# Transposing the first keys as fp32 on TensorE, a contiguous token-mixing weight in batch 0, and an uneven split of the last output piece

## The chip, the cores and the metric

The kernel runs on one core of a Trainium2 chip. A core has TensorE (PE, the matmul array), VectorE (DVE), ScalarE (ACT), GpSimd (POOL) and SyncE (SP, which here only issues transfers), each with its own instruction stream, run in order. SP, ACT and POOL start DMA transfers. Matmuls write PSUM, eight banks of 128 partitions by 2 KB; [...]everything else lives in SBUF. The metric is the device time of one execution in microseconds (us): 292.88 for the kernel before, the median of three runs from 292.81 to 293.12.

## What is computed

Performer attention with positive random features, and on its output one token- and channel-mixing MLP block. With 8 batches, 8 heads, 576 tokens, head size 64 and 128 features:

```python
def phi(x):                                  # x scaled by D ** -0.25
    proj = np.einsum('bhsd,md->bhsm', x, omega)
    sq = np.sum(x * x, axis=-1, keepdims=True) / 2.0
    h = proj - sq
    h = h - np.max(h, axis=-1, keepdims=True)
    return np.exp(h) / np.sqrt(m)
kv = np.einsum('bhsm,bhsd->bhmd', k_p, v)
z = np.sum(k_p, axis=2)
x = num / den                                # num = q_p kv, den = q_p z + 1e-6; heads side by side: 576 x 512
h = np.maximum(xt @ w_tok1, 0.0) @ w_tok2    # xt = x transposed, w_tok 576 x 256 and 256 x 576
u = x + h.transpose(0, 2, 1)
h2 = np.maximum(u @ w_ch1, 0.0) @ w_ch2      # 512 x 1536 and 1536 x 512
out = u + h2
```

Inputs and output are fp32; the kernel computes in fp16 with fp32 sums in PSUM.

## The kernel before

**Tiling.** Of each batch's 576 tokens, 512 are the main part, four blocks j of 128, and 64 are the tail; the tails of two batches share one set of 128 partitions. In SBUF, partition p of block j holds token 4p + j, since loads put four neighbouring tokens on one partition. Heads go in four pairs, hp = 0 to 3; the output of a pair fills 128 of the 512 columns, called db.

**The order.** A planner in the kernel (class `Planner`) takes jobs with an engine, an assumed cost, a due key, the jobs they depend on and the buffers that they take and give (six PSUM banks, one PSUM pair, rings of SBUF tiles). It writes out each engine's instructions once, in an order that follows from costs and keys; on the chip that order is fixed. The tables `KEYS`, `NEAR`, `HEAD` and `BY` hold the keys, and for batch 0 which engine (A for ScalarE, D for VectorE) takes which copy out of PSUM. Where PE would have nothing to do before the first channel mix, the planner inserts matmuls of zeros (L908).

**The opening, batch 0.** All that the change touches but the last piece lies here.
- `load_first` (L375) brings the fp32 keys in four transfers of two heads each, two issued by ACT and two by SP, into `first_k`, a view of the space that the weights `wc2` take later. A ScalarE copy (L381) casts each to fp16 in `nat`.
- `transposes` (L459) turns two heads with four TensorE transposes (L465): the data are the loaded weights and an identity is the moving operand. L470 (ACT) or L472 (DVE) copies the result from PSUM to `kT`. `tail_transposes` (L485, L489) does this for the tail tokens. POOL makes the fp16 identity at L387.
- For each pair: `kp` (L611) multiplies keys by the features, L494 on ACT takes the exponential, L637 and L639 on DVE the maximum per token and its reciprocal, L644 on POOL scales v, `kv` (L657, L664) sums over tokens, and L672 copies the sums out. `qp` (L625) and its exponentials (L494) do the same for the queries, `num` (L691, L693) forms numerator and denominator, and L700 and L701 on DVE divide them into x. Where `BY["no"]` has an A, L710 takes the reciprocal on DVE and ACT does the division in five pieces (L713).
- `token_mix_first` (L760) then takes each db: the first token matmul t1 (L771, L772), a relu (L778 on ACT or L780 on DVE), and a group of PE work that forms u transposed in one bank: four identity matmuls (L787) put x in, transposed, and two matmuls with w_tok2 as the moving operand (L789) add the second token product. L793 copies the bank to `uT`. L789 reads w_tok2 through a view that reorders its columns,

```python
    def w2_of(tb, j=None):
        rows = w2[:, tb, 0:SM].rearrange("p (c j) -> p j c", j=NJ)
        return rows if j is None else rows[:, j, :]
```

so that bank column 128j + c is token 4c + j.
- The first `channel_mix` matmuls (L828, L830) start when `uT` is there; from then on PE has dense work. L822 is the first channel product, L839 its relu on ACT, L855 the second, L864 on DVE adds u (L861 copies for batch 0, whose u is added by L853 on PE), and L869 stores the block.

**The body.** Batches 1 to 7 run the same steps interleaved with the channel mix of the batch before. From batch 2 on, q and k are cast by a POOL transfer to DRAM (L354) and transposed by a DMA on SP's queue (L362).

**The end.** A ninth channel mix takes the tails. Its last block j = 3 is done in two column halves of 256, each with 12 matmuls L855, one add L864 and two stores L872 of 64 partitions, one issued by SP and one by ACT.

Of the kernel before, what the change touches and what calls it, by code (L numbers as in the profile page):

```python
# [9 lines left out]
FP32 = mybir.dt.float32  # L10
# [6 lines left out]
KEYS = {"a": -1.383, "as": 0.1, "t": -0.936, "ts": 0.381, "gv": 2.163, "lt": -2.027, "lv": -2.126, "to": -1.882, "tt": 0.315, "ks": 0.333, "km": 0.498, "vs": -0.625, "l1": -2.543, "kt": -0.025}  # L17
NEAR = {"1": {"a": -1.493, "as": 0.086, "t": -1.525, "ts": 0.0, "gv": -0.107, "km": -1.714, "vs": -0.23, "kt": -0.097}, "2": {"a": -1.272, "as": 0.154, "t": -0.7, "ts": 0.142, "gv": 1.686, "km": 3.516, "vs": 1.881, "lv": -1.598, "lt": -2.533, "kt": 0.06}}
HEAD = {"kp": [-3.838, -3.822, -3.798, -3.404], "ke": [-2.728, -2.927, -2.827, -2.727], "km": [-4.011, -3.564, -4.193, -4.006], "vs": [-3.332, -3.487, -3.03, -3.14], "qp": [-3.503, -3.403, -3.303, -3.203], "qe": [-3.328, -3.374, -3.028, -3.128], "kv": [-3.45, -3.145, -2.92, -3.05], "ko": [-3.015, -2.969, -3.397, -2.755], "n": [-3.199, -3.199, -3.182, -3.099, -2.999, -2.999, -2.899, -2.899], "no": [-3.34, -3.34, -3.24, -3.058, -3.14, -4.038, -3.04, -2.3], "ktm": -3.64, "kt": -5.015, "kte": -3.991, "qt": -3.751, "qte": -4.062, "kx": [-6.595, -5.9, -5.8, -5.7], "kxo": [-6.013, -7.195, -5.8, -5.71], "ktx": -6.15, "ktxo": -5.5, "qx": [-5.449, -2.792], "qxo": [-4.557, -3.081], "qtx": -5.58, "qtxo": -3.371, "t1": [-0.475, -0.755, -0.539, -0.445], "re": [-0.554, -0.394, -0.244, -0.084], "ut": [-0.17, -0.48, -0.32, -0.64], "uo": [-0.453, -0.293, -0.302, 0.017], "vbd": -8.94, "w1": -9.59, "w1t": -9.68, "w2t": -8.94, "wa": -8.32, "wb": -8.79, "w2": -8.13}
BY = {"kx": "DDDD", "ktx": "A", "qx": "AD", "qtx": "D", "ko": "ADDA", "re": "AADA", "uo": "DAAA", "no": "DDDDDDDD"}  # L20
# [157 lines left out]
def kernel(  # L178
# [12 lines left out]
    nc = tc.nc  # L191
# [3 lines left out]
    DM = H * D  # L195
# [20 lines left out]
    def sb(shape, dt, name):  # L216
        return pool.tile(shape, dt, name=name)
# [13 lines left out]
    omT = sb([P, M], FP16, "omT")  # L231
    ident16 = sb([P, P], FP16, "ident16")
# [71 lines left out]
    def dma(eng, key, wire, fn, deps=(), take=(), give=(), cost=None):  # L304
        cost = (0.75 if eng == "POOL" else 0.45) if cost is None else cost
        job = add(eng, cost, key, fn, deps, take, give, wire=wire)
        if eng == "POOL":
            job.after = issued[-1] if issued else None
            issued.append(job)
        return job  # L310
# [64 lines left out]
    def load_first(h0, h1, eng, key, to):  # L375
        def go():
            (nc.sync if eng == "SP" else nc.scalar).dma_start(
                out=first_k[:, h0:h1, :], in_=k[0, h0:h1, 0:SM, :].rearrange("h (p j) d -> p h (j d)", j=NJ))
        got = dma(eng, key, 0.37 * (h1 - h0), go, cost=0.47)
        def cast():  # L380
            (nc.vector.tensor_copy if to == "DVE" else nc.scalar.copy)(out=nat["k", 0][:, h0:h1, :], in_=first_k[:, h0:h1, :])  # L381
        job = add(to, 0.6 if to == "DVE" else 0.5, key + 0.1, cast, deps=[got])
        for h in range(h0, h1):
            ld["k", 0, h] = job

    def identities():
        make_identity(nc, ident16)  # L387
    j_ident = add("POOL", 0.45, -9.9, identities)
    j_om = [dma("SP", -9.95, 0.1, lambda: nc.sync.dma_start(out=omega_nat, in_=omega))]
    load_first(0, 2, "ACT", -9.9, "ACT")  # L390
    load_first(2, 4, "SP", -9.9, "ACT")
    load_first(4, 6, "ACT", -9.7, "ACT")
    load_first(6, 8, "SP", -9.7, "ACT")
# [27 lines left out]
    def w2_of(tb, j=None):  # L421
        rows = w2[:, tb, 0:SM].rearrange("p (c j) -> p j c", j=NJ)
        return rows if j is None else rows[:, j, :]
# [35 lines left out]
    def transposes(b, w, h0, h1, key, on_act=False, key_out=None):  # L459
        name = ("t", w, b, h0)  # L460
        def go():
            ps, ident = bank16(name), ident16
            for i in range(2 * (h1 - h0)):
                h, pr = h0 + i // 2, i % 2
                nc.tensor.transpose(ps[:, i * P : (i + 1) * P], nat[w, b][:, h, pr * P : (pr + 1) * P], ident)  # L465
        def out_():
            n = h1 - h0
            ps = bank16(name)[:, 0 : n * R].rearrange("p (h r) -> p h r", h=n)
            if on_act:
                nc.scalar.copy(out=rows_of(b, w)[:, h0:h1, 0:R], in_=ps)  # L470
            else:
                nc.vector.tensor_copy(out=rows_of(b, w)[:, h0:h1, 0:R], in_=ps)  # L472
        take = [("bank", name)]
        take.append((w + "T", b))
        t = add("PE", mm(2 * (h1 - h0), P) * 1, key, go, deps=[ld[w, b, h0], j_ident], take=take)
        e = add("ACT" if on_act else "DVE", 0.1 + 0.21 * (h1 - h0) if on_act else 0.16 + 0.13 * (h1 - h0), key if key_out is None else key_out, out_, deps=[t], give=[("bank", name)])
        for h in range(h0, h1):
            tr[w, b, h] = e
# [281 lines left out]
    def token_mix_first(b, key, step, jx):  # L760

        jrs, uT = [], []
        for db in range(ND):
# [20 lines left out]
            def ut_(n2=n2, cols=cols):  # L784
                ps, x, r1 = bank(n2), t_x[place("x", b)], t_r1[place("r1", b)]
                for j in range(NJ):
                    nc.tensor.matmul(ps[:, j * P : (j + 1) * P], x[:, j, cols], ident16, start=(j == 0), stop=False, skip_group_check=True)  # L787
                for tb in range(NT):
                    nc.tensor.matmul(ps, r1[:, tb, cols], w2_of(tb), start=False, stop=(tb == NT - 1), skip_group_check=True)  # L789
# [23 lines left out]
    def channel_mix(c, key, jt):  # L813
# [27 lines left out]
        for j in range(NJ):  # L841
            last = c == B and j == NJ - 1
            for hf in range(2 if last else 1):
                n = ("h4", c, j, hf)
                cols = slice(hf * (DM // 2), (hf + 1) * (DM // 2)) if last else slice(0, DM)
                prev = None
                for part in range(3):
# [8 lines left out]
                    prev = add("PE", mm(4, 256 if last else 512) + (mm(4, P) if c == 0 and part == 2 else 0.0), key + 0.5 + 0.5 * (3 * j + part) / 12 + 0.2 * hf, c2,  # L856
# [8 lines left out]
                jo = add("DVE", 0.4 if last else 0.69, k2, oadd, deps=[prev], take=[("o", (c, j))], give=[("bank", n)] + ([("u", c)] if 0 < c < B else []))  # L865
                def store(j=j, cols=cols, last=last):
                    o = t_o[place("o", (c, j))]
                    if c < B:
                        nc.sync.dma_start(out=out[c, 0:SM, :].rearrange("(p j) d -> p j d", j=NJ)[:, j, :], in_=o)  # L869
                    else:  # L870
                        for i in range(2):
                            (nc.scalar if j >= 2 and i else nc.sync).dma_start(out=out[2 * j + i, SM:S, cols], in_=o[i * ST : (i + 1) * ST, cols])  # L872
# [68 lines left out]
```

## Time and profile before

| | us |
|---|---|
| median of three runs | 292.88 |
| the profiled execution | 292.57 |
| its span, first to last instruction | 290.8 |
| PE busy | 283.9 |
| ACT, DVE, POOL busy | 155.9, 145.3, 90.6 |
| first L828 | 28.07 |
| end of the last add (L864) | 287.43 |

The span is shorter than the time of its execution by what lies before the first and after the last instruction that the profile counts. A busy time of PE overlaps neighbouring matmuls, since the ends of matmuls are modelled; the chain of work that ended last steps from start to start and shows what a matmul really adds. In a line of a group, "out<-in" names tiles, then come shapes, types and count, busy time in us and mean in ns, and the idle time before it with what ended it. In a line of the chain the columns are start, length in us and the work.

### The profile page before, as it was taken

How to read it: one execution, taken by the hardware profiler on the slowest of the kernel's cores; microseconds unless marked ns; L12 is line 12 of the kernel's file. 1: busy time of each engine (PE TensorE's matmuls, PEld its weight loads, DVE VectorE, ACT ScalarE, POOL GpSimd, SP SyncE). 2: the span in 40 equal slices, each digit the busy share in tenths (PEclk: the TensorE clock that was granted, in tenths of full speed). 3: DMA queues.
4: the chain of work that ended last, by engine and by line, in shares of the span. 5: the costliest groups of instructions: out<-in, count | busy, mean ns of one | idle time of the engine just before them, and what ended most of it. 6: DMA issues, size and time to landing. Idle time of an engine off the chain costs nothing.

```text
span 290.8 us, 5502 instructions
## 1 busy us (share of the span) xinstructions
PE 283.9 (98%) x2210; PEld 141.7 (49%) x2210; DVE 145.3 (50%) x269; ACT 155.9 (54%) x305; POOL 90.6 (31%) x115
## 2 busy tenths in 40 slices
PE   7899999999999999999999999999999999999994
PEld 3465454445544544465445544554455444444443
DVE  4885843558449533756567446646465242111011
ACT  5963992098457553865466636753765501621700
POOL 8995740128006501550165014601421000000000
PEclk9999999999999999999999999999999999999998
DMA  8999999699964996999769976897711033003004
GB/s 192 193 197 195 202 228 172 98 246 175 177 108 108 186 152 125 180 171 202 113 129 182 197 114 113 159 221 115 152 72 39 0 72 147 0 18 144 2 20 124
DMA packets 75737, 39.57 MB, mean 136 GB/s; under 512 B 54976, under 2 KB 70720, under 8 KB 75328
## 3 DMA queue, kind: packets, MB, share of 16 engines
q0 software_dynamic: 24304, 17.43, 41.2%
q1 hardware_dynamic: 50624, 21.01, 32.3%
q10 hardware_dynamic: 784, 0.79, 0.9%
q8 instruction: 17, 0.28, 0.4%
q14 instruction: 8, 0.07, 0.1%
HBM read 35.88 MB, written 16.52 MB: 180 GB/s over the span
## 4 chain that ended last, share of the span: by engine, by line
PE 95%; ACT 3%; DVE 0%; issue 0%; DVEq 0%; ACTq 0%
PE bank L855 33%; PE bank L822 32%; PE bank L745 4%; PE bank L728 4%; PE bank L611 3%; PE bank L657 3%; PE bank L625 2%; PE pair L691 2%; PE bank L908 2%; ACT kp L494 1%; PE bank L789 1%; PE bank L803 1%; PE bank L664 1%; PE bank L465 1%; PE bank L729 1%; ACT qp L494 1%
## 5 line engine op out<-in xcount | busy, mean ns | idle before, releaser
L839 ACT ACTIVATE r<-bank 128x512 f16<-128x512 f32 x108 | 64.5, 602 | 69.8 <-PE bank L822 69.8
L855 PE MATMUL bank<-wc,r 128*128 128x512 f16 (+1 forms) x444 | 101.5, 374 | 0.0
L822 PE MATMUL bank<-uT,wc 128*128 128x512 f16 x376 | 89.5, 379 | 0.0
L855 PEld LDWEIGHTS <-r 128*128 128x128 f16 x444 | 40.8, 98 | 46.9 <-issue 5.1
L822 PEld LDWEIGHTS <-wc 128*128 128x128 f16 x424 | 39.5, 98 | 42.6 <-issue 0.5
L637 DVE TENSOR_REDUCE km<-kp 128x8 f16<-128x1024 f16 x32 | 38.7, 1209 | 9.4 <-ACT kp L494 9.2
L494 ACT ACTIVATE qp<-bank 128x512 f16<-128x512 f32 x64 | 35.2, 620 | 13.4 <-PE bank L625 13.4
L494 ACT ACTIVATE kp<-bank 128x512 f16<-128x512 f32 x64 | 34.4, 610 | 8.9 <-PE bank L611 8.9
L644 POOL TENSOR_TENSOR vs<-v,vs 128x512 f16<-128x512 f16 x32 | 33.4, 1055 | 16.1 <-DVE vs L639 12.1
L864 DVE TENSOR_TENSOR o<-u,bank 128x512 f32<-128x512 f16 x28 | 19.1, 681 | 28.1 <-PE bank L855 28.1
L571 POOL TENSOR_TENSOR vbd<-vt,vbd 128x1024 f16<-128x1024 f16 x7 | 13.4, 1919 | 33.2 <-DVE vbd L562 21.7
L365 POOL COPY ktt<-kT 128x256 f16<-128x256 f16 x6 | 2.4, 396 | 68.4 <-DMA kT<-k 68.4
L701 DVE TENSOR_TENSOR x<-pair,rc 128x640 f16<-128x640 f32 x28 | 23.1, 824 | 1.0
L748 DVE TENSOR_TENSOR u<-x,bank 128x512 f16<-128x512 f16 x28 | 17.4, 682 | 9.1 <-PE bank L745 9.1
L700 DVE RECIPROCAL rc<-pair 128x10 f32<-128x10 f32 x28 | 6.0, 216 | 26.9 <-PE pair L693 26.9
L691 PEld LDWEIGHTS <-qp 128*128 128x128 f16 x256 | 12.8, 98 | 6.1 <-issue 0.7
L736 DVE TENSOR_SCALAR r<-bank 128x512 f16<-128x512 f32 x7 | 4.8, 692 | 19.5 <-PE bank L729 19.5
L728 PE MATMUL bank<-x,w1m 128*128 128x512 f16 x56 | 14.4, 379 | 0.0
L657 PEld LDWEIGHTS <-kp 128*128 128x128 f16 x256 | 10.9, 98 | 5.3 <-ACT qp L494 0.9
L657 PE MATMUL bank<-vs,kp 128*128 128x65 f16 x256 | 13.0, 193 | 0.4 <-ACT qp L494 0.4
L745 PE MATMUL bank<-r,w 128*128 128x512 f16 x56 | 13.2, 379 | 0.0
L611 PE MATMUL bank<-omT,kT 64*128 64x128 f16 x256 | 12.5, 218 | 0.1
(102 smaller groups left out, 267.8 us busy)
## 6 DMA issues: line engine op xcount, KB each, us to landing
out_dram<-o SPq DMA_DIRECT2D x32, 256.0 KB, 2.5
q<-in_q_dram POOLq DMA_DIRECT2D x6, 576.0 KB, 6.5
k<-in_k_dram POOLq DMA_DIRECT2D x6, 576.0 KB, 10.2
wc<-in_moe_w_ch_dram POOLq DMA_DIRECT2D x4, 768.0 KB, 10.3
v<-in_v_dram POOLq DMA_DIRECT2D x6, 512.0 KB, 6.3
r<-in_q_dram POOLq DMA_DIRECT2D x4, 256.0 KB, 7.2
v<-in_v_dram POOLq DMA_DIRECT2D x4, 256.0 KB, 7.2
out_dram<-o SPq DMA_DIRECT2D x5, 128.0 KB, 2.3
```

What stands on the lines that cost most here:

```text
L494: nc.scalar.activation(out=out, in_=in_, func=AF.Exp, bias=0.0, scale=1.0)
L611: nc.tensor.matmul(ps[e][:, c : c + M], m[half[e], r, :], omT[half[e]], start=True, stop=True)
L637: nc.vector.reduce_max(out=mx, in_=kpv, axis=AX.X)
L644: nc.gpsimd.tensor_tensor(out=vs[:, :, 0:D], in0=t_v[place("v", b)][:, hh[0] : hh[0] + 2, :].rearrange("p h (j d) -> p (h j) d", d=D), in1 ...
L657: nc.tensor.matmul(ps[:, i, :], kpv[:, 2 * i + j // 2, j % 2, :], vs[:, i * NJ + j, 0 : D + 1], start=(i == 0 and j == 0), stop=False, ski ...
L701: nc.vector.tensor_tensor(out=t_x[place("x", b)][:, :, (2 * hp + hs[0]) * D : (2 * hp + hs[0] + n) * D].rearrange("p j (i d) -> p i j d", ...
L728: nc.tensor.matmul(ps, w1m[:, j, tb * P : (tb + 1) * P], x[:, j, :], start=(j == 0), stop=False)
L745: nc.tensor.matmul(ps, w2_of(tb, j), r1[:, tb, :], start=(tb == 0), stop=(tb == NT - 1))
L822: nc.tensor.matmul(ps, wc1[:, db, cb * P : (cb + 1) * P], moving(db), start=(db == 0), stop=(db == ND - 1))
L839: nc.scalar.activation(out=t_r3[place("r3", c)][:, cb, :], in_=bank(n), func=AF.Relu)
L855: nc.tensor.matmul(ps[:, cols], r3[:, cb, j * P : (j + 1) * P], wc2[:, cb, cols], start=(cb == 0), stop=(cb == NCB - 1))
L864: nc.vector.tensor_tensor(out=t_o[place("o", (c, j))][:, cols], in0=uu[:, cols], in1=bank(n)[:, cols], op=ALU.add)
```

## The change

It has three parts, and the planner's tables come with them.

1. Batch 0's w_tok2 is read as it lies. The identity matmuls L787 write the bank in steps of four columns instead, so that bank column t is token t; blocks j of `uT` are then 128 neighbouring tokens, and batch 0's output rows are stored in that order.
2. The ScalarE casts of batch 0's keys are gone. TensorE transposes the fp32 keys with an fp32 identity into an fp32 bank, and the DVE copy out of it casts to fp16. POOL makes the fp32 identity, and DVE copies it to fp16 for the other uses.
3. The last block's columns are split 384 and 128 instead of 256 and 256.

The tables change keys in `KEYS`, `NEAR` and `HEAD` (for batch 0 of `kp`, `qp`, `kxo`, `qxo` and `wb`), and in `BY` the tail keys' copy moves to DVE, the last pair's kv copy to DVE, the relus all to ACT, and the first head's division to ACT.

```diff
-BY = {"kx": "DDDD", "ktx": "A", "qx": "AD", "qtx": "D", "ko": "ADDA", "re": "AADA", "uo": "DAAA", "no": "DDDDDDDD"}
+BY = {"kx": "DDDD", "ktx": "D", "qx": "AD", "qtx": "D", "ko": "ADDD", "re": "AAAA", "uo": "DAAA", "no": "ADDDDDDD"}
...
-    def load_first(h0, h1, eng, key, to):
+    def load_first(h0, h1, eng, key):
...
-        got = dma(eng, key, 0.37 * (h1 - h0), go, cost=0.47)
-        def cast():
-            (nc.vector.tensor_copy if to == "DVE" else nc.scalar.copy)(out=nat["k", 0][:, h0:h1, :], in_=first_k[:, h0:h1, :])
-        job = add(to, 0.6 if to == "DVE" else 0.5, key + 0.1, cast, deps=[got])
+        job = dma(eng, key, 0.37 * (h1 - h0), go, cost=0.47)
...
-        make_identity(nc, ident16)
-    j_ident = add("POOL", 0.45, -9.9, identities)
+        make_identity(nc, ident32)
+    j_ident32 = add("POOL", 0.45, -9.9, identities)
+    j_ident = add("DVE", 0.2, -9.9, lambda: nc.vector.tensor_copy(out=ident16, in_=ident32), deps=[j_ident32])
...
-    def w2_of(tb, j=None):
-        rows = w2[:, tb, 0:SM].rearrange("p (c j) -> p j c", j=NJ)
-        return rows if j is None else rows[:, j, :]
+    def w2_of(tb, j):
+        return w2[:, tb, 0:SM].rearrange("p (c j) -> p j c", j=NJ)[:, j, :]
...
+        first = b == 0 and w == "k"
         def go():
-            ps, ident = bank16(name), ident16
+            ps = bank(name) if first else bank16(name)
+            what, ident = (first_k, ident32) if first else (nat[w, b], ident16)
             for i in range(2 * (h1 - h0)):
                 h, pr = h0 + i // 2, i % 2
-                nc.tensor.transpose(ps[:, i * P : (i + 1) * P], nat[w, b][:, h, pr * P : (pr + 1) * P], ident)
+                nc.tensor.transpose(ps[:, i * P : (i + 1) * P], what[:, h, pr * P : (pr + 1) * P], ident)
         def out_():
             n = h1 - h0
-            ps = bank16(name)[:, 0 : n * R].rearrange("p (h r) -> p h r", h=n)
+            ps = (bank(name) if first else bank16(name))[:, 0 : n * R].rearrange("p (h r) -> p h r", h=n)
...
                 for j in range(NJ):
-                    nc.tensor.matmul(ps[:, j * P : (j + 1) * P], x[:, j, cols], ident16, start=(j == 0), stop=False, skip_group_check=True)
+                    nc.tensor.matmul(ps.rearrange("p (c j) -> p j c", j=NJ)[:, j, :], x[:, j, cols], ident16, start=(j == 0), stop=False, skip_group_check=True)
                 for tb in range(NT):
-                    nc.tensor.matmul(ps, r1[:, tb, cols], w2_of(tb), start=False, stop=(tb == NT - 1), skip_group_check=True)
+                    nc.tensor.matmul(ps, r1[:, tb, cols], w2[:, tb, 0:SM], start=False, stop=(tb == NT - 1), skip_group_check=True)
...
-                cols = slice(hf * (DM // 2), (hf + 1) * (DM // 2)) if last else slice(0, DM)
+                cols = (slice(0, 3 * P), slice(3 * P, DM))[hf] if last else slice(0, DM)
...
-                        nc.sync.dma_start(out=out[c, 0:SM, :].rearrange("(p j) d -> p j d", j=NJ)[:, j, :], in_=o)
+                        rows = out[c, 0:SM, :]
+                        rows = rows.rearrange("(p j) d -> p j d", j=NJ)[:, j, :] if c else rows[j * P : (j + 1) * P, :]
+                        nc.sync.dma_start(out=rows, in_=o)
```

In the changed kernel's order on PE, the four blocks of key transposes stand as: three of them without a pause, then kp of pair 0, the fourth block, the tail keys, kp of pairs 1, 2 and 3. The numerators of pairs 0 and 1 and kv of pair 3 stand ahead of the first t1. Lines below L229 of the changed kernel are shifted by one or two; the matmuls of zeros are L910 there.

## The prediction

> **What bounds the kernel now.** I read the busy shares first, then the chain of work that ended last in order of time, then the groups by shape in the opening 30 us, and last the queue of the final stores.
>
> ```profile
> PE 283.9 (98%) x2210; PEld 141.7 (49%) x2210; DVE 145.3 (50%) x269; ACT 155.9 (54%) x305; POOL 90.6 (31%) x115
> ```
>
> TensorE is busy for 98% of the span, and after 28 us the table of waits shows no wait of PE at all. So the time is: when PE reaches the first channel-mix matmul (L828), plus a dense body, plus the tail. The chain shows what comes before L828 (start, length, work):
>
> ```profile
> 3.69 0.85 PE bank L908 x2
> 4.54 0.57 PE bank L465 x4
> 5.12 0.43 PE bank L908
> 5.54 0.43 PE bank L465 x4
> ...
> 7.20 1.56 ACT kp L494 x3
> 8.77 0.26 ACT ktt L489
> 9.03 1.48 ACT kp L494 x3
> 10.51 0.90 ACT qT L470
> 11.41 1.04 ACT kpt L538 x4
> 12.45 1.95 ACT qp L494 x4
> ...
> 18.13 0.38 PE bank L771 x4
> ...
> 22.80 0.22 PE bank L787 x4
> 23.02 0.90 PE bank L789 x2
> ...
> 28.07 0.75 PE bank L828 x3
> ```
>
> Three stages are to be seen: PE and its warm-up matmuls (L908) to 6.7 us; ScalarE, back to back from 7.20 to about 18 us on its exponentials; PE again, dense from 18.13 to 28.07 but for two L908 (0.43). And L789 takes 0.45 us a matmul, while L728 with as many columns takes 0.86 for four, 0.215. L789 alone reads its moving operand with a step of four elements.
>
> **The change, part by part.**
>
> *The body* after L828. Both built programs hold the same instructions there in almost the same order; on PE, two matmuls L625 and two L586 swap places with their neighbours, so that the switches between half-height and full-height matmuls fall from 70 to 68. A switch costs 0.11 (L822 x4 takes 0.97 after an L611 and 0.86 otherwise): between 0 and -0.2, I take **-0.1**. Batch 0's stores write 2 KB rows as before and lie under PE's work. The body moves as a block with L828 unless a load holds it: the transposed q of batch 2, the nearest I found, lands at 53.4 (issued 45.05, 8.3 to landing) and is first read at 57.5, 4 us of slack.
>
> *w2 contiguous.* Eight L789 fall from 0.45 to 0.215: 8 x 0.235 = -1.88 of PE time. Against it, 16 identity matmuls L787 (0.22 for four, 0.055 each) now write PSUM with a step of four fp32. No row shows a stepped PSUM write. The Trainium skill speaks against it (PSUM — Partial Sum Buffer, Specifications): a PSUM line is 8 bytes, and any non-contiguous pattern slows matmuls significantly. With free writes one u-transposed group (four L787, two L789) costs 0.22 + 0.43 = 0.65, against 1.12 now; with one write per line, twice the time as the stepped read has it, 0.43 + 0.43 = 0.86; at four times, 1.31. I take 0.86, by the nearest row, the stepped read's factor of two.
>
> *Keys as fp32.* Gone are four ScalarE casts (0.618 each). In their place stand 16 fp32 transposes and slower evacuations:
>
> ```profile
> L381 ACT CAST r<-wc 128x512 f16<-128x512 f32 x4 | 2.5, 618 | 1.8 <-DMA wc<-in_k_dram 1.7
> L472 DVE COPY kT<-bank 128x512 f16<-128x512 f16 x4 | 1.7, 424 | 2.6 <-PE bank L465 2.6
> L793 DVE CAST uT<-bank 128x512 f16<-128x512 f32 x1 | 0.7, 691 | 0.6 <-PE bank L789 0.6
> ```
>
> L793 is an evacuation of the new shape and types, so each of the four goes from 0.42 to 0.69. The first cast ran at 3.84 under the two L908 that hold PE until 4.54; those stay, so the first transposes start at 4.54 as before, and this cast's removal gains nothing. An fp16 transpose cost 0.107 here (0.43 for four at 5.54, PE still at half pace though the clock row reads full) and 0.055 later. For fp32 there is no row. By the Trainium skill (TensorE: Matmul & The Clock Gate, Terms and Weight-path perf modes) transpose mode makes FP32 four times faster than its matmul, which I read as one pass, but FP32 has no fast weight load. So the load, which the fp16 row hides, is added: I estimate twice the row, 0.21 until about 6.1 us and 0.12 after. The ends: the fp16 price, and four passes with an open load (4 x 0.055 + 0.107 = 0.33 late, twice that early).
>
> Now the order of the new program, with those prices:
> - PE: two blocks of four transposes, 4.54 to 6.22 at 0.21 (their keys had landed when the casts started, 3.84 and 4.6), the third 6.25 to 6.75 (landed by 5.3), kp for pair 0 to 7.1. First exponential at 7.2: no change.
> - DVE evacuates at 5.45, 6.3, 7.0 and 7.7, 0.69 each, then the tail keys (0.42, moved from ScalarE) to 8.8. PE: fourth block (landed 6.66) to 7.6, tail to 7.85, kp pair 1 to 8.2. ScalarE needs that at 7.2 + 2 x 0.52 = 8.25, so it runs on without a hole. Queued behind these evacuations are the key maxima: the first starts at 8.8 as now, kt_nb ends at 10.9 and is wanted at 11.8.
> - ScalarE's sum to the last query exponential: 8 kp x 0.52, qT 0.90, kpt 1.04, 8 qp x 0.49, qpt 0.54, plus, new here, one kvsb 0.27 and one head's normalisation in five pieces of about 0.21 (estimate from kpt's 0.26 at twice the columns): 11.9, less the tail-key copy of 0.26. It ends at 19.1, 1.1 later than now. Only pair 2 waits for it.
> - The last kp exponential ends at 15.6 (15.4 now). DVE: maximum and reciprocal 1.4, to 17.0; one head of pair 0, 0.68; two kvsb, to 18.4. PE: numerators of pair 1 at 18.5, kv of pair 3 to 19.15. DVE: pair 1's heads to 20.0, pair 2's to 21.4, kvsb, uT copy, pair 3's heads to 24.0.
> - PE from 19.15: t1 0.57, numerators 0.30, one L910 0.22, t1 0.56, group 0.86 (21.66), t1 0.56, numerators 0.30, two groups (24.24; DVE's last x at 24.0 is just in time), t1 0.56, sixteen L465 0.90 (as at 25.61 now), group 0.86 (26.56), tail and kp of batch 1 0.44: **L828 at 27.0** against 28.07, **-1.07**.
>
> In words: at 18.13 PE had 9.5 us of work left plus 0.43 of L908; the new one has 8.3, 0.2 of L910 and 0.4 of holes.
>
> POOL's identity is now fp32, and a DVE cast (about 0.2, before DVE's wait for omega at 3.12) makes the fp16 one. POOL's memset and select grow by at most their own 0.50, so its loads issue up to 0.5 later. The first q load lands some 5.6 after 3.59, at 9.2, and is wanted near 9.5; ScalarE takes the result at 10.4. A delay of 0.5 is covered by that; without the cover it would cost 0.1 to 0.3.
>
> *The last piece.* Now:
>
> ```profile
> 287.01 0.42 DVE L864 TENSOR_TENSOR o<-ut,bank 128x256 f32<-128x256 f16 x1 [0.80 <-PE bank L855]
> 287.46 0.47 SPq L872 DMA_DIRECT2D out_dram<-o  x1
> ```
>
> With 384 and 128 columns PE's sum stays (12 x 0.1625 + 12 x 0.056 = 2.62). The last add shrinks to 0.28 and ends at 287.29 instead of 287.43. But the 384-column add runs 286.34 to 286.89, so its store holds SP's queue from 286.92 for 0.55, and ScalarE's for 0.50 to 0.74: the last store issues at 287.47 and at up to 287.66, against 287.46 and 287.5. Gain 0.14, given back to the queue: **0**, between -0.15 and +0.15.
>
> **Sum.** The profiled execution took 292.57 with a span of 290.8, so 1.77 lie outside. 290.8 - 1.07 - 0.1 + 0 = 289.6; plus 1.77 is 291.4. The median of the runs is 0.31 above the profiled one: **291.7**, or 1.2 less than 292.88.
>
> **Rivals.**
> 1. *Stepped writes cost nothing, or the transposes are nearly as cheap as fp16's.* Then the group costs 0.65, DVE's last x (24.0) sets the end, and L828 comes at 26.5: 291.2. For: four accumulating fp32 writes are not a read. Against: the stepped read's factor.
> 2. *The gain goes to small costs.* Writes at three times their price (groups 1.08: L828 at 27.9), or PE staying at half pace beyond 6.1 because the L908 between the transposes is gone: 292.7 in the middle. For: each hand-over between engines costs some 0.05 and I summed some thirty. Against: PE is dense from 19.15, which hides most of them.
> 3. *The slower side: FP32 transposes in four passes.* The place is 4.54 to the second pair's exponentials. At 0.33 (0.66 early) the three blocks take 1.56 us for some two and a half transposes and 9.5 x 0.33 = 3.1 for the rest: end 9.2, first exponential 9.65, 2.4 late; the fourth block (1.3) then stands ahead of kp pair 1 and opens a hole of 0.8 on ScalarE. 3.2 late less 1.2 gained is 2.0 slower, 294.9; with the load hidden (0.22, 0.43 early) the delay is 1.6 and the time 293.3. In the middle 294.1. Written with p as the mean price of the sixteen, the delay is 12p - 2.21 and the hole 4p - 0.51; they eat the 1.2 gained at p = 0.24, and from there it decides. For: nothing in the trace shows an fp32 operand on PE.
>
> **How the numbers follow.** What a measurement of this kernel cannot tell from no change is within 0.2%, 292.3 to 293.5. As summed, 291.7 (own range 291.2 to 292.3): 0.50. Rival 1: 0.14. Rival 2: 0.16, of which 0.14 within the band. Rival 3: 0.20, nearly all above it. So faster 0.65, same 0.15, slower 0.20. The range: below 290.9 only rival 1 with everything free (0.05), above 294.0 half of rival 3 (0.10): 290.9 to 294.0.
>
> **What would show it.** L465 on the fp32 keys stepping by 0.21 and then about 0.12 (rival 3: 0.33 or more); first kp exponential at 7.2; no hole on ScalarE up to 15; L787 at 0.11 a step (rival 1: 0.055); L789 at 0.215; L828 at 27.0; last add 0.28 long, last SP store no earlier after PE's end than now. The prediction is wrong if the first exponential starts after 8.3, or if L787 steps by more than 0.18, or if a load makes PE wait after 28 us.

## The result, and the profile after

The changed kernel takes 291.63 us (median of four runs, 291.38 to 292.21) against 292.85 (292.68 to 293.12) for the kernel before on the same chip: a ratio of 0.996, 95% interval 0.9943 to 0.9978. Forecast: 291.7. Its profiled execution took 291.51 with a span of 289.7, 1.1 less than before. Run again beside a later set of the kernel before, it gave 291.54 against 292.63, 0.9958 (0.9946 to 0.9971).

The first part of the profile page, busy time by engine: PE has 1.5 us less, DVE 0.8 more and ACT 1.6 less, but all three are sums over the span and say nothing of what was worth what.

```profile
PE 282.4 (97%) x2207; PEld 143.3 (49%) x2207; DVE 146.1 (50%) x270; ACT 154.3 (53%) x305; POOL 90.5 (31%) x115
```

The chain that ended last in the first 31 us of the changed kernel (start, length, work) can be laid against the chain in the prediction:

```profile
1.67 5.22 DMA wc<-in_k_dram
...
10.08 0.91 ACT qT L470
...
12.51 1.95 ACT qp L494 x4
...
18.75 0.22 PE bank L771 x4
...
20.40 0.44 PE bank L787 x4
20.84 0.43 PE bank L789 x2
...
26.63 0.75 PE bank L828 x3
```

Two marks cut the time into pieces that can be compared from run to run: the copy of the first transposed queries (qT, L470), which ScalarE does between two exponentials, and the first L828.

| us | before | after | difference |
|---|---|---|---|
| start to the qT copy | 10.51 | 10.08 | -0.43 |
| qT copy to L828 | 17.56 | 16.55 | -1.01 |
| L828 to the start of the last add | 258.94 | 258.74 | -0.20 |
| start of the last add to the end of the span | 3.77 | 4.34 | +0.57 |
| span | 290.78 | 289.71 | -1.07 |

(The page rounds a span to 0.1; the table takes the end of each trace to 0.01.) The chain now begins with a load: the fourth key block lands at 6.88 and PE waits for it. L787 takes 0.44 for four where it took 0.22, L789 0.43 for two where it took 0.90.

The first row of the table has three causes. In the kernel before, the cast of the fourth key block stood ahead of the first exponential in ScalarE's order and waited for its load:

```profile
6.68 0.62 ACT L381 CAST r<-wc 128x512 f16<-128x512 f32 x1 [0.71 <-DMA wc<-in_k_dram]
```

So the first exponential started at 7.20, though kp of pair 0 had ended at 6.31. In the changed kernel no cast holds it; it follows kp of pair 0 and starts at 6.76, 0.44 earlier. Between it and the qT copy ScalarE no longer copies the tail keys (0.26; the new table gives that copy to VectorE), and a hole that has come in takes back some 0.3.

One row of the groups by shape in the first 28 us of the changed kernel (busy us, mean ns of one, idle time before and its cause) gives the evacuation L472, 688 ns with the cast in it:

```profile
L472 DVE CAST kT<-bank 128x512 f16<-128x512 f32 x4 | 2.6, 688 | 1.8 <-PE bank L465 1.8
```

And the end of the changed kernel, from the timeline (start, length, engine; the "q" rows are an engine busy issuing a transfer):

```profile
285.34 0.74 ACTq L874 DMA_DIRECT2D out_dram<-o  x1
285.37 0.29 DVE L864 TENSOR_TENSOR o<-ut,bank 128x128 f32<-128x128 f16 x1
285.89 0.55 SPq L874 DMA_DIRECT2D out_dram<-o  x1
286.18 0.56 ACTq L874 DMA_DIRECT2D out_dram<-o  x1
```

The last add ends at 285.66, but ScalarE is still issuing the store of the 384-column piece until 286.08. Its last store starts 0.52 after the add has ended; before, it started 0.04 after (287.43 and 287.47). From the start of the last add to this issue it is 0.81, where it was 0.46. From the issue to the landing it is 2.4, where it was 2.2 (before, then changed; KB, and us to landing):

```profile
out_dram<-o ACTq DMA_DIRECT2D x1, 64.0 KB, 2.2
out_dram<-o ACTq DMA_DIRECT2D x1, 32.0 KB, 2.4
```

These 0.35 and 0.2 are the whole of the 0.57, since from this landing to the end of the span it is 1.1 in both. Why the smaller store lands later is not shown.

### The profile page after: what moved, and what is told of

The parts are those of the page before. It is cut to its first block, busy times and chain, and to the rows that moved or that the text cites. A ratio compares the mean times of both kernels' runs of the same rounds, so it can differ in the third digit from the quotient of the medians.

```text
span 289.7 us, 5498 instructions
## 1 busy us (share of the span) xinstructions
PE 282.4 (97%) x2207; PEld 143.3 (49%) x2207; DVE 146.1 (50%) x270; ACT 154.3 (53%) x305; POOL 90.5 (31%) x115
## 4 chain that ended last, share of the span: by engine, by line
PE 93%; ACT 3%; DMA 2%; issue 0%; SPq 0%; DVE 0%; DVEq 0%
PE bank L855 33%; PE bank L822 32%; PE bank L745 4%; PE bank L728 4%; PE bank L611 3%; PE bank L657 3%; PE bank L625 2%; PE pair L691 2%; DMA wc<-in_k_dram 2%; PE bank L803 1%; PE bank L664 1%; PE bank L729 1%; ACT qp L494 1%; PE bank L465 1%; ACT kp L494 1%; PE bank L771 1%
## 5 line engine op out<-in xcount | busy, mean ns | idle before, releaser
L855 PE MATMUL bank<-wc,r 128*128 128x512 f16 (+2 forms) x444 | 101.5, 374 | 0.0
```

What stands on the lines that cost most here:

```text
L855: nc.tensor.matmul(ps[:, cols], r3[:, cb, j * P : (j + 1) * P], wc2[:, cb, cols], start=(cb == 0), stop=(cb == NCB - 1))
```

## The experiments

Each kernel was run beside the kernel before on the same chip (medians of before 292.61, 292.57 and 292.63 in the three sets). Times are medians; spans and marks are from a kernel's one profile.

### One part undone

**Halves again.** The changed kernel with the last piece in 256 and 256 columns.

```diff
-                cols = (slice(0, 3 * P), slice(3 * P, DM))[hf] if last else slice(0, DM)
+                cols = slice(hf * (DM // 2), (hf + 1) * (DM // 2)) if last else slice(0, DM)
...
```

> The changed kernel with its last piece split 256 and 256 again, all else alike. Theory Q (the two queues are held by the 384 columns' stores, so that the last store starts late): in the changed kernel the last add ends 285.66 and the span 289.7, 4.0 us later, against 3.4 in the kernel before; with halves the 4.0 becomes 3.4 while the add is 0.13 longer, so 0.5 us faster than the changed kernel, about 291.1, 1.7 under the kernel before. Rival, the forecast's sum: the split is worth nothing, 291.6. ScalarE's last store should issue within 0.1 us of the end of the last add (Q), not 0.5 after it.

Measured: 291.18, ratio 0.9955 (0.9942 to 0.9968), span 289.0. The timeline of this kernel's end, and one row of its opening chain:

```profile
284.82 0.74 ACTq L874 DMA_DIRECT2D out_dram<-o  x1
285.27 0.42 DVE L864 TENSOR_TENSOR o<-ut,bank 128x256 f32<-128x256 f16 x1 [0.80 <-PE bank L855]
285.73 0.50 ACTq L874 DMA_DIRECT2D out_dram<-o  x1
```

```profile
4.79 1.66 PE bank L465 x12
```

ScalarE's store of the first half takes as long (0.74), but it has half the columns' time to do it in and is through at 285.56, before the last add ends (285.69). From the start of the last add to the end of the span it is 3.73, against 4.34 with 384 and 128: in the trace the split costs 0.6. ScalarE's last store lands 2.2 after its issue here, as before. In whole times the gain over the kernel before is 1.43 here, 1.22 and 1.09 in the two sets of the changed kernel, and the intervals (some 0.4 to each side) overlap, so the times alone would not tell the two apart.

**The read stepped again.** The changed kernel with the old layout of w_tok2's columns: L787 writes its bank contiguously, L789 reads in steps of four.

```diff
-                    nc.tensor.matmul(ps.rearrange("p (c j) -> p j c", j=NJ)[:, j, :], x[:, j, cols], ident16, start=(j == 0), stop=False, skip_group_check=True)
+                    nc.tensor.matmul(ps[:, j * P : (j + 1) * P], x[:, j, cols], ident16, start=(j == 0), stop=False, skip_group_check=True)
...
-                    nc.tensor.matmul(ps, r1[:, tb, cols], w2[:, tb, 0:SM], start=False, stop=(tb == NT - 1), skip_group_check=True)
+                    nc.tensor.matmul(ps, r1[:, tb, cols], w2[:, tb, 0:SM].rearrange("p (c j) -> p j c", j=NJ), start=False, stop=(tb == NT - 1), skip_group_check=True)
...
-                        rows = rows.rearrange("(p j) d -> p j d", j=NJ)[:, j, :] if c else rows[j * P : (j + 1) * P, :]
+                        rows = rows.rearrange("(p j) d -> p j d", j=NJ)[:, j, :]
```

> The changed kernel with w_tok2 read in steps of four again and the identity matmuls writing without steps, in the same order of instructions. Theory: PE sets the end of the opening, and a u-transposed group goes from 0.87 back to 1.12 us. All four groups lie on its way: 4 x 0.25 = 1.0 slower than the changed kernel, 292.6. Rival 1: VectorE's last x sets the end, and the groups have slack: the one group behind it counts, and at most 0.25 is lost, 291.9.

Measured: 292.91, ratio 1.0009 (1.0 to 1.0017), span 291.5. Its opening chain:

```profile
4.79 2.56 PE bank L465 x12
...
10.82 0.91 ACT qT L470
...
21.15 0.22 PE bank L787 x4
21.37 0.90 PE bank L789 x2
...
28.41 0.75 PE bank L828 x3
```

From the qT copy to L828 it is 17.59, against 16.55 in the changed kernel and 17.56 before: the contiguous w_tok2 is worth 1.04 on the path, and the new tables, which stay here, change nothing between these marks on balance. Of the 1.78 by which L828 is later than in the changed kernel, the other 0.74 lie ahead of the qT copy, where this edit does nothing. There the twelve transposes took 2.56 where the same twelve, which enter the chain at the same 4.79, took 1.66 with the halves. That is taken up at the end.

**Both contiguous.** L787 writes contiguously and L789 reads contiguously. The token order of batch 0's x within u is then not the right one: the reordering is left out, the work is otherwise the same.

```diff
-                    nc.tensor.matmul(ps.rearrange("p (c j) -> p j c", j=NJ)[:, j, :], x[:, j, cols], ident16, start=(j == 0), stop=False, skip_group_check=True)
+                    nc.tensor.matmul(ps[:, j * P : (j + 1) * P], x[:, j, cols], ident16, start=(j == 0), stop=False, skip_group_check=True)
```

> The changed kernel with the identity matmuls writing without steps and w_tok2 read without steps, so that in batch 0 x is added to the wrong tokens: the token order of x in batch 0 is left out. It measures what the stepped write costs. Theory: identity matmuls go from 0.11 to 0.055 us, a group from 0.87 to 0.65. Three groups stand before the last t1, which started at 23.87 with VectorE's last x ready at 23.36: 0.5 of their 0.66 can be had, and 0.22 of the last group, 0.7 in all, 290.9. If PE alone sets the end: 0.88, 290.75. If VectorE alone does: 0.22, 291.4.

Measured: 291.14, ratio 0.9951 (0.9938 to 0.9964), span 289.0. Its chain:

```profile
9.86 0.91 ACT qT L470
...
20.18 0.22 PE bank L787 x4
20.40 0.43 PE bank L789 x2
...
25.76 0.75 PE bank L828 x3
```

The qT copy to L828 takes 15.90, 0.65 less than in the changed kernel. Sixteen L787 at 0.055 instead of 0.11 make 0.88, so three quarters of the stepped writes' price show. This is what part 1 pays for its own gain.

### One suspected cost doubled

Each fp32 transpose is done twice.

```diff
-                nc.tensor.transpose(ps[:, i * P : (i + 1) * P], what[:, h, pr * P : (pr + 1) * P], ident)
+                for _ in range(2 if first else 1):
+                    nc.tensor.transpose(ps[:, i * P : (i + 1) * P], what[:, h, pr * P : (pr + 1) * P], ident)
```

> The changed kernel with every fp32 key transpose done twice, into the same place: 16 more of 0.11 (0.17 to 0.2 early). It moves the mean price of a transpose from 0.17 to about 0.3, past the 0.24 where rival 3 of the forecast turns the gain. Theory (ScalarE's exponentials carry a late start to the end of the opening): the first exponential goes from 6.76 to about 8.1, that of pair 1 from 8.02 to about 9.4; 1.3 slower than the changed kernel, 292.9, no better than the kernel before. Rival (the dense stage of PE takes up half of a late start): 292.2.

Measured: 293.67, ratio 1.0035 (1.0023 to 1.0047), span 291.4.

```profile
4.79 3.18 PE bank L466 x24
...
8.30 1.02 PE bank L466 x8
...
11.82 0.91 ACT qT L471
...
28.37 0.75 PE bank L829 x3
```

Slower than the kernel before by 0.35%. The changed kernel's second run, below, is the one to compare with, since its transposes enter the chain at the same point (4.78): there the qT copy comes at 10.25 and L828 at 26.79. Here they come 1.57 and 1.58 later, and between the two it is 16.55 against 16.54. The delay is made of the transposes themselves: 24 in 3.18 for twelve in 2.05, 1.13 more, and 8 in 1.02 for four in 0.66, 0.36 more, together 1.49. So what the fp32 transposes cost is carried on whole by ScalarE's row of exponentials, and nothing after it takes any of it up. Done twice, the mean price of what was one transpose is (3.18 + 4 x 0.22) / 16, about 0.25. The rival of slow FP32 transposes was to eat the gain at 0.24; L828 is 0.30 later than before here, and the last piece's split adds its 0.5. The mechanism and its turning point hold, and the price in the changed kernel is the low one. Whole times show more than the traces: by medians this kernel is 2.1 slower than the changed kernel's second run (293.67 against 291.54), by the two spans 1.6; its profiled execution was the fastest of its five.

### One part alone

Three kernels start from the kernel before.

**w_tok2 alone** (batch 0's rows stored in token order; the old tables stay):

```diff
-                    nc.tensor.matmul(ps[:, j * P : (j + 1) * P], x[:, j, cols], ident16, start=(j == 0), stop=False, skip_group_check=True)
+                    nc.tensor.matmul(ps.rearrange("p (c j) -> p j c", j=NJ)[:, j, :], x[:, j, cols], ident16, start=(j == 0), stop=False, skip_group_check=True)
...
-                    nc.tensor.matmul(ps, r1[:, tb, cols], w2_of(tb), start=False, stop=(tb == NT - 1), skip_group_check=True)
+                    nc.tensor.matmul(ps, r1[:, tb, cols], w2[:, tb, 0:SM], start=False, stop=(tb == NT - 1), skip_group_check=True)
...
```

> The kernel before with w_tok2 contiguous in batch 0 and the identity matmuls writing in steps, nothing else, in the same order of instructions. Theory: each of the four groups takes 0.87 instead of 1.12, PE is dense from 18.13 us to L828: 1.0 faster, 291.85. Rival: VectorE's x or the relus hold it, since there the last x was only just in time (23.12 against 23.92): 0.5 to 0.7 faster, 292.3.

Measured: 292.06, ratio 0.998 (0.9971 to 0.9989), span 290.4. The chain:

```profile
1.21 4.03 DMA wc<-in_k_dram
5.27 0.63 ACT r L381
...
11.11 0.90 ACT qT L470
...
27.73 0.75 PE bank L828 x3
```

The qT copy to L828: 16.62, 0.94 less than before. The whole opening came 0.60 late in this profile, because the second key load landed at 5.24 and its cast waited for it; before, that cast started at 4.6.

**fp32 keys alone**: the changed kernel with the edits of "halves again" and "the read stepped again", and the four tables of the kernel before, of which the last is

```diff
-BY = {"kx": "DDDD", "ktx": "D", "qx": "AD", "qtx": "D", "ko": "ADDD", "re": "AAAA", "uo": "DAAA", "no": "ADDDDDDD"}
+BY = {"kx": "DDDD", "ktx": "A", "qx": "AD", "qtx": "D", "ko": "ADDA", "re": "AADA", "uo": "DAAA", "no": "DDDDDDDD"}
...
```

> The kernel before with the keys transposed as fp32, nothing else, with the tables of the kernel before, so that the tail keys' copy stays on ScalarE and no division moves there. Theory: casts gone, the first exponentials 0.4 earlier as in the changed kernel, and the opening ends 0.4 earlier: 292.45. Rival (the gain of the changed kernel is the contiguous w_tok2 alone, and the fp32 keys are neutral): 292.85. Third, the longer VectorE copies hold the maxima: 293.2.

Measured: 292.02, ratio 0.9985 (0.9974 to 0.9995), span 290.2, L828 at 27.62, 0.45 earlier than before. The marks do not serve here: the planner put one exponential fewer ahead of the qT copy than in the other kernels, and the chain ahead of L828 runs through POOL, with batch 1's first query load issued between two scalings of v:

```profile
14.18 0.88 POOL r L317
...
15.07 1.08 POOL vs L644
...
27.62 0.75 PE bank L828 x3
```

So fp32 keys with the old tables do not show what fp32 keys bring with the new ones.

**The split alone:**

```diff
-                cols = slice(hf * (DM // 2), (hf + 1) * (DM // 2)) if last else slice(0, DM)
+                cols = (slice(0, 3 * P), slice(3 * P, DM))[hf] if last else slice(0, DM)
...
```

> The kernel before with the last piece split 384 and 128, nothing else. Theory Q (queues held by the larger store): 0.5 slower, 293.35. Rival, the forecast's sum: no change, 292.85. A third, that the shorter last add counts: 0.14 faster, 292.7.

Measured: 293.37, ratio 1.003 (1.0019 to 1.0041), so slower by 0.56 to 1.20; from the last add's start to the end it takes 4.25. Six traces with halves (before, halves again, w_tok2 alone, fp32 alone and the last two below) have 3.73 to 3.77 there; seven with 384 and 128 columns (all others but the one in which POOL stores) have 4.16 to 4.34. The split is a loss of some 0.5, in both kernels.

By the stages the parts add up: -0.94 for w_tok2 between the qT copy and L828, -0.45 for fp32 keys on all that lies ahead of L828, +0.5 for the split: -0.9, against -1.07 of which -0.20 is the body, in which neither part alone has its order. By whole times they do not: -0.51, -0.55 and +0.80 make -0.26, where each has an interval of some 0.3 to either side and the changed kernel gained 1.1 to 1.2. In the one trace of w_tok2 alone 0.60 of its gain is lost to a late load; whether that happened in its other runs, no trace tells.

**Casts again, new tables.** The changed kernel with ScalarE's casts and fp16 keys, to see what the tables do without fp32.

```diff
-        job = dma(eng, key, 0.37 * (h1 - h0), go, cost=0.47)
+        got = dma(eng, key, 0.37 * (h1 - h0), go, cost=0.47)
+        job = add(to, 0.6 if to == "DVE" else 0.5, key + 0.1, cast, deps=[got])
...
```

> The changed kernel with its keys cast on ScalarE and transposed as fp16 again; contiguous w_tok2, the 384 and 128 split and the new tables stay, and the planner draws its order anew. Theory (fp32 keys and their order give 0.4 to 0.7 of the gain): 292.2. Rival (they give nothing): 291.6.

Measured: 295.22, ratio 1.0092 (1.0078 to 1.0106). The chain ahead of L828 runs elsewhere:

```profile
16.96 11.07 DMA r<-in_k_dram
...
28.08 1.07 PE bank L464 x16
```

With the casts in place the planner wrote another order, in which POOL issues the load of batch 1's keys at 16.96, behind its scalings of v. It landed at 28.03 and PE stood before batch 1's key transposes. This run says nothing of the casts; how much of the gain the tables bring by themselves stays open.

### The changed kernel again, and three attempts at more

The changed kernel a second time:

> The changed kernel itself, for a comparison on the same chip with the three beside it. 0.996 of the kernel before, 291.4 to 291.7; the last add starts 4.3 us before the end of the span, where kernels with halves have 3.7.

Measured: 291.54, span 289.8. ScalarE's first six exponentials in its timeline, and two marks of its chain:

```profile
7.20 3.05 ACT L494 ACTIVATE kp<-bank 128x512 f16<-128x512 f32 x6 [4.14 <-PE bank L611]
```

```profile
10.25 0.90 ACT qT L470
...
26.79 0.75 PE bank L828 x3
```

From qT to L828: 16.54. Here the first exponential starts at 7.20, as before the change, and the six follow without a hole. The qT copy comes 0.26 earlier than before, which is the copy of the tail keys that has moved to VectorE; the fp32 keys bring nothing ahead of this mark. In the first profile they brought 0.44 at the first exponential and lost some 0.3 of it in the hole. So what they are worth depends on when their transposes start and when they get to full pace, and no run prices them alone.

**The 384-column piece stored by POOL,** so that the queues of SP and ScalarE are free when the last add ends:

```diff
-                            (nc.scalar if j >= 2 and i else nc.sync).dma_start(out=out[2 * j + i, SM:S, cols], in_=o[i * ST : (i + 1) * ST, cols])
+                            (nc.gpsimd if last and cols.start == 0 else nc.scalar if j >= 2 and i else nc.sync).dma_start(out=out[2 * j + i, SM:S, cols], in_=o[i * ST : (i + 1) * ST, cols])
```

> The changed kernel with the two stores of its 384-column piece issued by POOL, which is idle then, so that SP and ScalarE are free when the last 128 columns are added. Theory Q (the held queues cost the split its gain): SP and ScalarE issue the last stores within 0.1 us of the last add's end, 0.2 and 0.5 earlier than now; from the start of the last add to the end of the span 3.6 us instead of 4.3, so 0.6 to 0.7 faster than the changed kernel. Rival (small packets of 512 bytes or the number of transfers in flight set the end, not the queues), or POOL's own stores landing last: 4.2 us or more, and the same time.

Measured: 292.76, ratio 1.0003 (0.9992 to 1.0013), span 291.3: no gain but a loss of about 1.2 against the changed kernel. Its end in the timeline:

```profile
286.01 0.29 DVE L864 TENSOR_TENSOR o<-ut,bank 128x128 f32<-128x128 f16 x1
286.18 0.60 POOL L874 DMA_DIRECT2D out_dram<-o  x1 [67.67 <-DVE o L864]
286.33 0.50 ACTq L874 DMA_DIRECT2D out_dram<-o  x1
286.77 0.58 POOL L874 DMA_DIRECT2D out_dram<-o  x1
```

ScalarE issues its last store at 286.33, 0.03 after the add has ended (286.30), instead of 0.52 after: that the store in front held the queue is shown. But the queue was not all. POOL starts its first store 0.30 after the 384-column add (its end: 285.88), is busy with the two until 287.35, and then the end of the span comes 4.00 later, against 2.97 after ScalarE's last store in the changed kernel. ScalarE's last store, though issued 0.49 earlier after the add's start, takes 3.0 to land instead of 2.4, so it lands no earlier: a free queue alone gained nothing while the larger piece was still being stored. POOL's second store lands last, 2.7 after its issue, at 289.5, and from there to the end it is 1.9, where it is 1.1 in the changed kernel. What these further 0.8 are is not shown. From the last add's start to the end it takes 5.34 instead of 4.34. Another 0.47 of this profile is the opening, where the fourth key block landed at 7.36.

**The fourth key block behind kp of pair 1** (and halves), so that PE need not stand before a load:

```diff
+            if b == 0 and hp == 1:
+                plan.move = (jobs_t["k", 0, 6], j_k)
...
-            j.fn()
+            if j is not self.move[0]:
+                j.fn()
+            if j is self.move[1]:
+                self.move[0].fn()
...
```

> The changed kernel with halves as in the first experiment, and the fourth block of key transposes behind kp of pair 1 on PE; every other order is kept. In the changed kernel PE waits for that block's keys (landed 6.88) with kp of pair 1 queued behind it, and ScalarE has a hole from 7.8 to 8.0. Theory: without the hole the copy of the queries starts at 9.8 instead of 10.0 to 10.1: 0.2 to 0.3 faster than halves alone, and 0.7 to 0.9 faster than the changed kernel. Rival: kp of pair 3, which needs the block, opens the same hole later: halves' gain alone, 0.5.

Measured: 291.79, ratio 0.9967 (0.9955 to 0.9979), span 289.7. No gain over the halves alone (291.18). Its chain:

```profile
5.68 1.90 DVE kT L476 x3
...
7.62 0.38 PE bank L615 x7
...
8.62 0.70 DVE kT L476
...
9.37 0.40 PE bank L615 x8
...
10.58 1.01 ACT qT L474
```

kp of pair 1 starts its last seven matmuls at 7.62, hardly earlier than with the block ahead of it (7.68 with the halves): what lets it go is the third evacuation on DVE, done at 7.58. The fourth block had stood in a gap of PE. Now its own evacuation ends at 9.33, kp of the last pair waits for that, and the qT copy comes at 10.58 instead of 9.99.

**The same, and no zero matmuls (L910) between the transpose of omega and the first key block:**

```diff
-                            self.warm(i)
+                            if not any(j2 is j for j2 in self.bare):
+                                self.warm(i)
...
+    plan.bare = [jobs_t["k", 0, 0]]
...
```

> As the one before, and without the two matmuls of zeros that hold PE from 3.4 to 4.26 while the first keys landed at 3.84. Theory: the first transposes start 0.5 earlier, the first exponential at 6.3, and 0.2 to 0.4 more is gained, 1.1 in all against the changed kernel. Rival (PE stays at half pace for longer, since two of seven matmuls of zeros are gone): the third block's transposes step by 0.2 instead of 0.11, the first exponential at 6.8, nothing more than the one before.

Measured: 291.40, ratio 0.9953 (0.9942 to 0.9965), span 289.8. The first transpose starts 0.53 earlier than in the experiment before (4.05 against 4.58), and yet kp of pair 0 follows at 6.78 instead of 6.52:

```profile
4.05 2.81 PE bank L471 x12
```

With the last one's 0.44 taken off, 0.215 a step to the end: half pace. Whether the missing zero matmuls kept it at half pace is not settled by this, because with all zero matmuls in place the same twelve ran at half pace to the end in the run with the read stepped.

None of these beats the changed kernel with halves, and that one is ahead of the changed kernel by less than the times can tell.

## Why the prediction was right, step by step

The time was right; the working was right up to L828, but for its start in the first profile, and wrong at the end. In the changed kernel's second run the opening came as forecast, but for ScalarE's row, which was some 0.3 shorter.

- *fp32 transposes at 0.21, then 0.12.* Right: 0.21 a step from 4.26, 0.11 afterwards, twice the fp16 price that the chain before shows late (0.055). The reason given, one pass and a weight load that is not hidden, is not shown: in the run with both contiguous the loads last 0.14, longer than the step, so they do run beside the matmuls. Why the price is twice stays open. The forecast took the early step to hold until 6.1. In the first profile it ended at about 5.6, in the second run at about 6.1; this is not a property of the change.
- *The evacuation at 0.69.* 0.688.
- *First exponential at 7.2, no hole on ScalarE.* Both so in the second run (7.20, and none). That it is also the time of before is a coincidence of two paths, of which the forecast reckoned one: before, the fourth cast held ScalarE; now it is kp of pair 0. In the first profile it started at 6.76. The forecast let the first block begin at 4.54 as before; omega landed at 2.81 in this profile, so it began at 4.26, and the half pace ended sooner. Having begun earlier, ScalarE wanted pair 1 at 7.84 and waited to 8.02. PE finished kp of pair 1 at 8.00, earlier than the forecast's 8.2 but not by as much, since the fourth block landed at 6.88 and not at 6.66.
- *ScalarE's sum of 11.9 to the last query exponential.* 11.90 (6.76 to 18.66), but with the hole in it, which the sum did not have. Without one, in the second run, it is 11.63 (7.20 to 18.83): the sum was some 0.3 too long. One term of it, the kvsb copy, took 0.16 to 0.17 and not 0.27.
- *PE dense from 19.15 to L828 at 27.0*, 7.85. Measured 18.75 to 26.63, 7.88. L787 at 0.11 a step and L789 at 0.215 are the forecast's values. So the whole of the 0.37 by which L828 beat its forecast lies ahead of PE's dense stretch. In the second run it is 0.21, from ScalarE's shorter row.
- *The body, -0.1, between 0 and -0.2.* -0.20.
- *The last piece, 0, between -0.15 and +0.15.* This step failed: +0.57. The forecast had the two mechanisms, a shorter add and a store that holds the queue, but set one against the other. The shorter add is worth nothing when the queue is not free at its end. It took SP's (0.01 late) for the end and named ScalarE's "up to 287.66", 0.16 to 0.19 late; ScalarE's was 0.81 after the add's start, where it had been 0.46, since 0.10 pass between the end of the 384-column add and its store's issue, and 0.10 between that store's end and the next. These 0.35 are shown by the rows. The other 0.2 is the landing (2.4 from the issue, against 2.2 before and with the halves), for which the forecast had no term. That the held queue alone is the cause is not shown: with POOL storing the larger piece ScalarE's queue was free, and its last store landed no earlier.
- *The sum* came right (291.7 against 291.63 and 291.54) since the opening, 0.37 better than forecast, and the body, 0.1 better, stood against +0.57. That they cancel so nearly is luck, and so is a part of the rest: the forecast put the median 0.31 above the profiled execution, and it was 0.12 above it in the first set and level with it in the second.
- *Rival 1 (free writes, or transposes nearly at the fp16 price)*: false, 0.11 a step for both; the run with both contiguous prices the stepped write at 0.65. *Rival 2*: the half pace does go on past 6.1 in some runs, to 7.3 in the one with the stepped read; it was thought of as a consequence of the missing L908, and comes with that in place too: in the split alone, which has it, the eight matmuls of kp of pair 0 take 0.54 from 6.24, where they took 0.33 before. *Rival 3*: the price was the low one; doubled, it makes the kernel slower than before as it was reckoned.

## What to carry to other kernels

Here the step in a layout had to be paid somewhere: the stepped moving operand cost 2.1 times (0.45 against 0.215) on 512 columns and the stepped PSUM write 2 times (0.11 against 0.055), so the step belongs on the side with fewer columns in all. At the end of a kernel follow the last stores, queue by queue, to their issue and to their landing: an add shortened by 0.13 lost 0.57, since the larger piece was ready late, its store still held the queue (0.35), and the last store took longer to land (0.2). And cut a profile at marks that the change does not touch: from the qT copy to L828 five traces with the changed opening took 16.54 or 16.55, while the copy itself lay anywhere from 9.99 to 11.82.

## What the runs showed of the hardware that was not expected

*The moment at which TensorE goes from half to full pace differs from run to run, with the same instructions.* Twelve fp32 transposes that enter the chain at 4.78 or 4.79 took 1.66 with the halves, 2.05 in the changed kernel's second run, and 2.56 with the read stepped, in one order on PE. In the run with the read stepped, every one of the twelve lasts 421 ns, the last from 6.93 to 7.35; in the run with both contiguous none lasts over 328, from 4.37 on. The transposes of the keys in these two traces, one group of instructions each (the first four microseconds and what follows 7.4 left out):

```profile
L465 PE MATMUL bank<-ident,wc x12: 421/421/421, 4.6 to 6.9; 128*128 128x128 f32 x12
```

```profile
L465 PE MATMUL bank<-ident,wc x16: 272/273/328, 4.4 to 7.1; 128*128 128x128 f32 x16
```

(duration in ns, least, median and most, and the first and last start.) So the change came before 4.4 in one and after 7.3 in the other, while the row of granted clock reads 1.00 in both from the start. The Trainium skill (TensorE: Matmul & The Clock Gate, Part 1) has a rule that fits: the gate that doubles TensorE's clock looks at activity in a window of about 3.4 us that runs free of the kernel, so that its phase decides. The page puts the spread at 500 ns to either side; here it is some 3 us, nearly the window. No run here moved the window itself, and the clock row does not show it; the steps decide, and they show a lottery of up to 0.9 us that ScalarE then carries on: the qT copy came at 9.99 after the 1.66, 10.25 after the 2.05 and 10.82 after the 2.56.

*First loads land at different times too*: omega at 2.81 in the first profile of the changed kernel and at 3.1 to 3.3 in all others, the fourth key block at 6.59 to 7.36. Leaving out the doubled transposes and the moved fourth block, the qT copy ranged from 9.86 to 10.82 over six kernels' profiles with the changed opening, and from 10.51 to 11.11 over the three with the old one. That is nearly as much as this change was worth, which may be why the parts' medians do not add up and their stages nearly do.
